# Query features of batches 1 to 3: a and b repeated by DMA through DRAM, their products as matmul weights

## The chip, the cores and the metric

The kernel runs on one core of one Trainium2 chip. Times are device microseconds of that core for one whole execution; a profile shows one such execution, and its span is a little shorter than the time of the run.

## The reference

Two blocks are chained. The first is an attention without softmax, whose features are products of two projections; the second mixes eight experts with weights that are balanced in eight rounds over rows and columns.

```python
def phi(x):                                   # (4, 4, 1088, 32) -> (4, 4, 1088, 64)
    a = np.einsum('rd,bhsd->bhsr', S1, x)     # r = 8
    b = np.einsum('rd,bhsd->bhsr', S2, x)
    return np.einsum('bhsi,bhsj->bhsij', a, b).reshape(*x.shape[:-1], r * r)
q_p, k_p = phi(q), phi(k)
kv = np.einsum('bhsf,bhsd->bhfd', k_p, v)
z = np.sum(k_p, axis=2)
num = np.einsum('bhsf,bhfd->bhsd', q_p, kv)
den = np.einsum('bhsf,bhf->bhs', q_p, z)[..., None] + 1e-06
x = (num / den).transpose(0, 2, 1, 3).reshape(4352, 128)
...
logits = x @ w_gate
P = np.exp(logits - logits.max())
for _ in range(8):
    P /= P.sum(1, keepdims=True) + 1e-09
    P /= P.sum(0, keepdims=True) + 1e-09
    P *= N / E
for e in range(8):
    out += P[:, e:e + 1] * (np.maximum(x @ w1[e], 0.0) @ w2[e])    # w1[e] 128 x 1024
```

All data are float32 (S1 and S2 arrive as float64).

## The kernel before

**Layout.** x is kept transposed in `xT`: head and dimension on the 128 partitions, the 4352 tokens along the free axis, batch after batch of S = 1088.

**Attention of one batch** (L272 to L396). `transpose_k` and `transpose_q` turn k and q with VectorE. `keys_ab` projects the keys (TensorE, weights taken from kT), ScalarE copies the projections, `keys_products` multiplies them on VectorE, and `keys_sums` (L324) sums products times v and times ones into kv and z; `keys_kept` copies these to `kvz`. The queries go in three chunks of 384, 352 and 352 tokens, with features on partitions and tokens along the free axis: `query_products` (L355) computes a and b already repeated to 64 features a head, with 64 rows and 128 columns of the array, and ScalarE copies a to `qa`; `multiply` (L367) forms the products on VectorE; `fractions` (L377) multiplies by kv and, in a second bank, by z repeated over 32 columns; `divide` (L389 to L396) takes one denominator of 32 by a transpose, forms the reciprocal, repeats it by a second transpose and multiplies into `xT`.

**Experts.** `groups` lists which tokens and experts are computed together. Seven plain groups come first (expert 0 on all tokens, expert 1 on the first 1280); their results are kept and weighted later, so they need only x. They are computed two token tiles at a time in seven products (`seven`, L973) of sums of the hidden layer's blocks; then come weighted groups of three tiles, whose x is multiplied by the routing weights beforehand. In each step `first` (L800) computes one block of the hidden layer into a bank, ScalarE applies the relu (L804), VectorE forms the sums (L817 in plain groups, L862 in groups of three), and the second layer follows `LAG` = 8 steps behind. A step of a plain group of n columns counts n/480 units. Up to three weight sets are prepared ahead at the start of an item (`prepare_w`).

**Order.** The attention is a generator with a `yield` between stages; `fill(n)` runs expert steps worth n units between them, so that TensorE has plain-group work while an attention stage waits on another engine. `counts` gives the units for each yield. Batch 0's attention comes ahead of all experts; batch 1's begins among the first fills; then `routing` runs its eight rounds with fills in between. The order on TensorE and VectorE is as written (`manual_schedule`); for SP's queue and POOL the framework chooses it, mostly as written. [...]

**Banks.** The attention and `first` take turns in the four PSUM banks of tag "a" (`bank()`, one after the other round the ring); the other four hold the second layer's sums, and before them batch 0's query products.

**Loads.** k, q and v are loaded on SP's queue: one DMA each for k and q, twelve for v. `load_kq` and `load_v` for batch 0 come first, then k and q of batch 1, the gate, expert 0's weights and v of batch 1.

```python
    def load_kq(b):
        kx = ld.tile([P, SA, D], F32, tag="k", name="kx")
        qx = ld.tile([P, SA, D], F32, tag="q", name="qx")
...
    chunks = ((0, 384), (384, 736), (736, S))
...
    counts = {1: (1, 1, 1, 1, 1, 1, 1, 1, 1), 2: (1, 1, 1, 1, 1, 1, 1, 1, 1, 1, 1, 2),
              3: (1, 1, 1, 1, 1, 1, 1, 1, 1, 1, 1, 1.25)}
```

Of the kernel before, what the change touches and what calls it, by code (L numbers as in the profile page):

```python
# [50 lines left out]
def kernel(  # L51
# [73 lines left out]
    xT = big.tile([P, N], F32, name="xT")  # L125

    lgT = wk.tile([P, SA, 32], F32, name="lgT", bufs=1)
    lgp = wk.tile([P, SA, 32], F32, name="lgp", bufs=1)
# [3 lines left out]
    summed = []  # L132
    for i in range(2):
        t = consts.tile([P, 2, 2, 2, D], F32, name=f"kvz{i}")
        nc.vector.memset(t, 0.0)
        summed.append(t)
# [9 lines left out]
    def load_kq(b):  # L146
        kx = ld.tile([P, SA, D], F32, tag="k", name="kx")
        qx = ld.tile([P, SA, D], F32, tag="q", name="qx")
        nc.sync.dma_start(out=kx, in_=k[b].rearrange("h (s a) d -> (h s) a d", a=SA))
        nc.sync.dma_start(out=qx, in_=q[b].rearrange("h (s a) d -> (h s) a d", a=SA))  # L150
        loaded[b] = kx, qx, v_slots[b % 2]
# [15 lines left out]
    load_kq(0)  # L167
    load_v(0)
    load_kq(1)
# [65 lines left out]
    wq = consts.tile([P, 2, 2, R, R], F32, name="wq")  # L235

# [15 lines left out]

    wdf = wd.rearrange("p n h r -> p (n h r)")
# [8 lines left out]
    first_w = load_w(0)  # L262
    load_v(1)
# [4 lines left out]
    def products_bank(b, i):  # L268

        return bank() if b else mps.tile([P, 512], F32, tag=f"s{i}", name="s")  # L270

    def transpose_q(b, lo=0, hi=S):  # L272
        if not lo:
            queries[b] = wk.tile([P, S], F32, tag="qT", name="qT")
        nc.vector.transpose(out=queries[b][:, lo:hi], in_=loaded[b][1].rearrange("p a d -> p (a d)")[:, lo:hi])  # L275

    def transpose_k(b):
        kx = loaded[b][0]
        kT = wk.tile([P, S], F32, tag="kT", name="kT")
# [3 lines left out]
        keys[b] = kT  # L283

    def keys_ab(b):

        kT = keys[b]
        ab = wk.tile([P, 2, NT + 1, H * R], F32, tag="ab", name="ab")
# [25 lines left out]
    def keys_sums(b):  # L314

        kp, vx = products.pop(b), loaded[b][2]
# [14 lines left out]
    def keys_kept(b):  # L331
        pv = sums_of.pop(b)

        kvz = summed[b % 2]
        for i in range(2):
            for s in range(2):
                sl = slice(64 * s, 64 * (s + 1))
                if s:
                    nc.vector.tensor_copy(kvz[sl, :, i, s, :], pv[sl, i])
                else:  # L340
                    nc.scalar.copy(kvz[sl, :, i, s, :], pv[sl, i])
        keys[b] = kvz
# [3 lines left out]
    def query_products(b, c):  # L346
# [3 lines left out]
        qT = queries[b]  # L350
        banks = [[products_bank(b, 2 * i + m) for m in range(2)] for i in range(2)]
# [5 lines left out]
        ph = []  # L357
        for i in range(2):
            qa = wk.tile([P, 384], F32, tag=f"qa{i}", name="qa")
            nc.scalar.copy(qa[:, 0:n], banks[i][0][:, 0:n])  # L360
            ph.append((qa, banks[i][1]))
        queries[b, c] = ph

    def multiply(b, c):
        n = chunks[c][1] - chunks[c][0]
        for qa, pb in queries[b, c]:
            nc.vector.tensor_tensor(qa[:, 0:n], qa[:, 0:n], pb[:, 0:n], op=Alu.mult)  # L367

    def fractions(b, c):

        n = chunks[c][1] - chunks[c][0]
        kvz = keys[b]
        ph = queries[b, c]
        pn, pd = bank(), bank()
        for t, m in ((pd, 1), (pn, 0)):
            for i in range(2):
                nc.tensor.matmul(t[64 * i:64 * (i + 1), 0:n], kvz[:, (i + m) % 2, i].rearrange("p h d -> p (h d)"),  # L377
                                 ph[i][0][:, 0:n], start=True, stop=True, tile_position=(0, 64 * i))
        queries[b, c] = pn, pd

    def divide(b, c):
# [5 lines left out]
        pn, pd = queries.pop((b, c))  # L387
# [8 lines left out]
        nc.vector.tensor_tensor(xT[:, b * S + lo:b * S + hi], pn[:, 0:n], rd[:, 0:n], op=Alu.mult)  # L396
# [16 lines left out]
    def attention(b):  # L413
# [3 lines left out]
        if b > 1:  # L417
            query_products(b, 0)
            yield
            keys_sums(b)  # L420
            multiply(b, 0)
            if follows:
                transpose_k(b + 1)
            yield
            keys_kept(b)
            fractions(b, 0)
            yield
        divide(b, 0)
        if b + 2 < B:
            load_kq(b + 2)  # L430
            load_v(b + 2)
        if follows:
            keys_ab(b + 1)
        yield
        query_products(b, 1)
        yield
        multiply(b, 1)
# [3 lines left out]
        fractions(b, 1)  # L441
        yield
        divide(b, 1)
        if follows:
            keys_products(b + 1, 0)
        yield
        query_products(b, 2)
        yield
        multiply(b, 2)
        if follows:  # L450
            keys_products(b + 1, 1)
        yield
        fractions(b, 2)
        yield
        divide(b, 2)
        if follows:
            keys_products(b + 1, 2)
        yield
# [11 lines left out]
    def routing():  # L470

        yield 0.75
# [43 lines left out]
        for b in (1, 0, 2, 3):  # L516
# [14 lines left out]
    groups = [(0, 256, 2, [0], False), *((512 + 960 * i, 480, 2, [0], False) for i in range(4)),  # L531
              (512, 384, 2, [1], False), (0, 256, 2, [1], False)]
# [14 lines left out]
    def prepare_w(j):  # L547
# [4 lines left out]
        elif items[j - 1][1] == e:  # L552
            loaded_w[j] = loaded_w[j - 1]
# [429 lines left out]
    def steps():  # L983

        todo, sums_at, t = {}, {}, 0
        for k in range(len(blocks) + 5):
# [5 lines left out]
            if k < len(blocks):  # L992
# [3 lines left out]
                if q == 0:  # L996
                    for i in (j, j + 1, j + 2 if j + 2 < first_weighted else j):
# [137 lines left out]
```

## Time and profile before

| | |
|---|---|
| median of three runs | 944.45 us (944.32 to 944.78) |
| span of the profiled execution | 942.6 us (its run: 944.38 us) |
| matmul instructions | 7170 |
| TensorE's granted clock | 0.998 |
| DMA over the span | 113.07 MB, mean 120 GB/s |
| first weighted expert matmul | 207.5 us |

In the profile PE is TensorE's matmuls and PEld its weight loads, DVE is VectorE, ACT ScalarE, POOL GpSimd, SP the engine whose queue issues most DMAs. A timeline row gives the start, the length, the engine, the line and the operation with its tiles and shapes; "128*64" is the part of the array in use, 128 rows by 64 columns, and "x8" the number of instructions merged. A float32 matmul call is two instructions. The end of a matmul is modelled and its latency is part of its length, so rows overlap; the distance from start to start is what it takes of TensorE.

### The profile page before, as it was taken

What the parts mean: (1) busy time and instruction counts of PE and PEld (TensorE: products, weight loads), DVE (VectorE), ACT (ScalarE), POOL (GpSimd) and SP (SyncE); (2) the same over time, 40 slices, a digit from 0 to 9 for tenths busy, and PEclk for the clock granted to TensorE, in tenths of its full rate; (3) what the DMA queues carried; (4) which work ended last, traced back from release to release, by engine and by line L of the source; (5) the groups of instructions that cost most, each with busy time, mean ns of one, the idle gap of its engine ahead of it and who ended that gap; (6) DMA issues with size and microseconds to landing.
All of it is one profiled execution on the core that took longest, in us unless ns stands there. A gap on an engine that the chain in (4) does not pass through costs nothing.

```text
span 942.6 us, 18270 instructions
## 1 busy us (share of the span) xinstructions
PE 928.9 (99%) x7170; PEld 556.1 (59%) x7170; DVE 702.4 (75%) x1214; ACT 419.6 (45%) x894; POOL 191.6 (20%) x176
## 2 busy tenths in 40 slices
PE   8999999999999999999999999999999999999996
PEld 6553535566666666665555555555555555556896
DVE  7787679988778788677785756975767977768665
ACT  2444445555444454444544444544445444445443
POOL 1010000063467411040011100110110343321220
PEclk9999999999999999999999999999999999999999
DMA  6600000122433454444453443454343556453640
GB/s 190 189 1 1 2 1 1 59 71 85 129 107 124 155 195 138 140 146 151 129 144 126 159 138 117 136 151 163 116 137 124 158 167 205 142 180 90 175 145 12
DMA packets 86342, 113.07 MB, mean 120 GB/s; under 512 B 23888, under 2 KB 67920, under 8 KB 81904
## 3 DMA queue, kind: packets, MB, share of 16 engines
q1 hardware_dynamic: 85024, 111.74, 38.3%
q8 instruction: 56, 0.92, 0.4%
q10 hardware_dynamic: 1232, 0.16, 0.1%
q14 instruction: 30, 0.25, 0.1%
HBM read 99.03 MB, written 12.85 MB: 119 GB/s over the span
## 4 chain that ended last, share of the span: by engine, by line
PE 94%; DVE 4%; issue 1%; ACT 1%; POOL 0%; DVEq 0%; ACTq 0%; POOLq 0%
PE a L800 48%; PE s L973 41%; PE a L355 1%; PE a L377 1%; PE a L324 1%; PE a L114 1%; DVE hb L862 1%; DVE hb L817 0%; DVE pqg L862 0%; PE a L293 0%; DVE kp L309 0%; DVE qa L367 0%; DVE qT L275 0%; PE a L402 0%; DVE rd L394 0%
## 5 line engine op out<-in xcount | busy, mean ns | idle before, releaser
L800 PE MATMUL a<-xe,w 128*64 128x256 f32 (+1 forms) x2560 | 517.8, 470 | 0.0
L804 ACT ACTIVATE hb<-a 128x256 f32<-128x256 f32 (+3 forms) x392 | 192.2, 493 | 257.8 <-PE a L800 232.8
L804 ACT ACTIVATE hx<-a 128x256 f32<-128x256 f32 (+1 forms) x360 | 167.3, 465 | 212.6 <-PE a L800 191.5
L800 PEld LDWEIGHTS a<-xe,w 128*64 128x64 f32 x2560 | 210.0, 137 | 73.2
L973 PE MATMUL s<-hb,ws 128*64 128x256 f32 (+2 forms) x1312 | 235.3, 400 | 0.1
L973 PE MATMUL s<-hx,ws 128*64 128x256 f32 x1280 | 205.4, 379 | 0.9 <-DVE kept L629 0.9
L862 DVE TENSOR_TENSOR hb<-hb 128x512 f32<-128x512 f32 (+1 forms) x204 | 131.0, 653 | 97.2 <-ACT hb L804 92.6
L862 DVE TENSOR_TENSOR hx<-hx 128x512 f32<-128x512 f32 (+1 forms) x204 | 152.5, 757 | 66.5 <-ACT hx L804 61.6
L569 POOL TENSOR_TENSOR xe<-xT,xe 128x768 f32<-128x768 f32 (+2 forms) x41 | 83.6, 2040 | 569.0 <-DMA xe<-pT 367.4
L973 PEld LDWEIGHTS s<-hb,ws 128*64 128x64 f32 x1312 | 109.0, 137 | 111.8 <-issue 85.8
L973 PEld LDWEIGHTS s<-hx,ws 128*64 128x64 f32 x1280 | 107.2, 137 | 95.4 <-issue 72.4
L800 PE MATMUL a<-xT,w 128*64 128x480 f32 (+2 forms) x448 | 121.8, 506 | 1.0 <-DVE xT L396 0.9
L973 PE MATMUL s<-hb,w 128*64 128x256 f32 (+2 forms) x472 | 100.9, 423 | 1.0 <-DVE kept L629 1.0
L817 DVE TENSOR_TENSOR hb<-hb 128x480 f32<-128x480 f32 (+5 forms) x84 | 65.8, 786 | 14.1 <-PE s L973 6.9
L973 PE MATMUL s<-hx,w 128*64 128x256 f32 x384 | 68.4, 379 | 0.0
L800 PEld LDWEIGHTS a<-xT,w 128*64 128x64 f32 x448 | 44.2, 137 | 32.8 <-issue 18.1
L225 POOL TENSOR_TENSOR ws<-w 128x256 f32<-128x256 f32 (+1 forms) x70 | 58.9, 876 | 13.1 <-PE a L800 9.8
L973 PEld LDWEIGHTS s<-hb,w 128*64 128x64 f32 x472 | 43.6, 137 | 27.9 <-issue 12.2
L817 DVE TENSOR_TENSOR hx<-hx 128x256 f32<-128x256 f32 (+1 forms) x65 | 39.5, 612 | 24.3 <-ACT hx L804 23.1
L862 DVE TENSOR_TENSOR pqg<-hb 128x512 f32<-128x512 f32 x68 | 51.3, 795 | 0.0
L973 PEld LDWEIGHTS s<-hx,w 128*64 128x64 f32 x384 | 34.4, 137 | 10.1
L862 DVE TENSOR_TENSOR pqg<-hx 128x512 f32<-128x512 f32 x68 | 35.0, 554 | 0.0
(150 smaller groups left out, 490.3 us busy)
## 6 DMA issues: line engine op xcount, KB each, us to landing
w<-in_moe_w_dram SPq DMA_DIRECT2D x82, 512.0 KB, 5.0
ws<-ws SPq DMA_DIRECT2D x34, 1024.0 KB, 5.0
xe<-pT SPq DMA_DIRECT2D x34, 384.0 KB, 3.9
ws<-ws SPq DMA_DIRECT2D x12, 512.0 KB, 4.7
pb<-pT SPq DMA_DIRECT2D x6, 384.0 KB, 6.7
kx<-in_k_dram SPq DMA_DIRECT2D x4, 544.0 KB, 4.3
qx<-in_q_dram SPq DMA_DIRECT2D x4, 544.0 KB, 5.6
v<-in_v_dram SPq DMA_DIRECT2D x32, 64.0 KB, 4.3
```

The lines of the kernel that those rows point to most:

```text
L114: nc.tensor.matmul(warm[:, 0:P], ones, ones, start=True, stop=True)
L225: tc.keep_in_program_order(nc.gpsimd.tensor_tensor(ws[:, c:c + len(ns)], blocks(x), blocks(y), op=Alu.subtract if off else Alu.add))
L324: nc.tensor.matmul(pv[64 * s:64 * (s + 1), i], kp[0:n, H * t + h].rearrange("p i j -> p (i j)"), vx[0:n, slots[h], t, :], start=(t == 0 an ...
L355: nc.tensor.matmul(banks[i][m][:, 0:n], wqf[sl, m, :], qT[sl, lo:hi], start=True, stop=True, tile_position=(64 * i, 0))
L377: nc.tensor.matmul(t[64 * i:64 * (i + 1), 0:n], kvz[:, (i + m) % 2, i].rearrange("p h d -> p (h d)"), ph[i][0][:, 0:n], start=True, stop=T ...
L569: tc.keep_in_program_order(nc.gpsimd.tensor_tensor(out, x, pb, op=Alu.mult))
L800: nc.tensor.matmul(ph[sl], loaded_w[j][0][:, P * f + H2 * s:P * f + H2 * (s + 1)], sources[j][:, lo:hi], start=True, stop=True, tile_posit ...
L804: nc.scalar.activation(out=out, in_=ph, func=Act.Relu)
L817: nc.vector.tensor_tensor(out, a, b, op=Alu.subtract)
L862: nc.vector.tensor_tensor(out if not isinstance(out, tuple) else places(*out), places(*a), places(*b) if isinstance(b, tuple) else b, op=A ...
L973: nc.tensor.matmul(sums[g][i][H2 * s:H2 * (s + 1), n * place:n * (place + 1)], w, x, start=c == 1, stop=c == per, tile_position=(0, H2 * s))
```

## The change

Batch 0 is computed as before. For batches 1 to 3 the queries are handled with tokens on partitions at the end:

- `queries_ab` projects q with one set of weights (`wdq`) for four heads; for this the 1088 tokens are padded to 1152 (`W9` = 288 blocks in each of four quarters). It stores a once and b eight times over to DRAM (`qa`, `qb`); `repeat` loads both back so that each of a's and b's rows stands where the 64 features of a head need it, b in `rb`, a in `phs`.
- `times` multiplies them on VectorE, a third of the batch at a time (768 elements a partition).
- `tops` uses those products as weights and moves the keys' sums `kvs` (two heads of 32 columns and z, 66 columns), so numerators and denominators of 64 tokens come out together, tokens on partitions; two more matmuls with ones add the 1e-6.
- `over` takes one reciprocal for each token and head, multiplies, and transposes; `take_over` stores the result to DRAM and loads it back into `xT` in the layout needed.
- The two buffers of k become one; k of batch 1 is loaded after v of batch 1, k and q of later batches after `keys_ab` or `tops`. kT and qT have one buffer each and are shared with the logits' tiles.
- The plain groups have other sizes and another order (eight of them, the same pairs of token and expert), the fills between the attention's stages are 1.4 units, and `routing` begins with a fill of 5 units. Weights of the third item aren't prepared at the first.

The diff, cut:

```diff
-    xT = big.tile([P, N], F32, name="xT")
-    lgT = wk.tile([P, SA, 32], F32, name="lgT", bufs=1)
-    lgp = wk.tile([P, SA, 32], F32, name="lgp", bufs=1)
+    xT = big.tile([P, N + 2 * 32], F32, name="xT")
+    W9 = 9 * 32
+    qT = wk.tile([P, 4 * W9], F32, name="qT", bufs=1)
+    nc.gpsimd.memset(qT[:, S:], 0.0)
+    kT = wk.tile([P, S], F32, name="kT", bufs=1)
+    phs = [wk.tile([P, 2, 4 * W9], F32, name=f"ph{i}", bufs=1) for i in range(2)]
+    rb = wk.tile([P, 2, 4 * W9], F32, name="rb", bufs=1)
+    lgT = qT[:, 0:S].rearrange("p (a s) -> p a s", s=32)
+    lgp = kT.rearrange("p (a e) -> p a e", e=32)
...
+        kvs.append(consts.tile([P, 2, 2, D + 1], F32, name=f"kvs{i}"))
...
+    eps = consts.tile([P, 3, H], F32, name="eps")
+    nc.gpsimd.memset(eps, 1e-6 / P)
...
-    load_kq(0)
+    load_k(0)
+    load_q(0)
     load_v(0)
-    load_kq(1)
...
+        nc.gpsimd.tensor_copy(wdq[:, 0], wd[:, 0].rearrange("p h r -> p (h r)"))
+        nc.gpsimd.tensor_copy(wdq[:, 1].rearrange("p (r h) -> p r h", h=H), wd[:, 1].rearrange("p h r -> p r h"))
...
     first_w = load_w(0)
+    load_q(1)
     load_v(1)
...
+    def queries_ab(b):
+        qa = dram.tile([H * R, 2, 2 * W9], F32, name=f"qa{b}")
+        qb = dram.tile([R, R * H, 2, 2 * W9], F32, name=f"qb{b}")
+        ab = wk.tile([P, 3, 192], F32, tag="qab", name="qab", bufs=1)
+        x = qT.rearrange("p (h q c t s) -> p h c t q s", h=2, q=2, c=3, t=3)
+        for cs in ((0, 1), (2,)):
+            pq = bank()[:, 0:192 * len(cs)].rearrange("p (c n) -> p c n", n=192)
+            for i, c in enumerate(cs):
+                for s in range(2):
+                    nc.tensor.matmul(pq[64 * s:64 * (s + 1), i].rearrange("p (t q s) -> p t q s", t=3, q=2),
+                                     wdq.rearrange("p n f -> p (n f)"), x[:, s, c], start=True, stop=True,
+                                     tile_position=(0, 64 * s))
+            nc.scalar.copy(ab[:, cs[0]:cs[-1] + 1], pq)
+        abf = ab.rearrange("p c n -> p (c n)")
+        for s in range(2):
+            nc.sync.dma_start(out=qb.rearrange("i f s n -> s f i n")[s],
+                              in_=abf[64 * s + 32:64 * (s + 1)].unsqueeze(1).to_broadcast([32, R, 2 * W9]))
+        for s in range(2):
+            nc.sync.dma_start(out=qa[:, s], in_=abf[64 * s:64 * s + 32])
+        queries[b] = qa, qb
+
+    def repeat(b):
+        qa, qb = queries.pop(b)
+        for h in range(2):
+            nc.sync.dma_start(out=rb[64 * h:64 * (h + 1)],
+                              in_=qb.rearrange("i (j x h) s n -> h (i j) x (s n)", x=2, h=2)[h])
+        for j in range(R):
+            nc.sync.dma_start(out=phs[b % 2][j::R], in_=qa.rearrange("(x r) s n -> r x (s n)", x=2))
...
+    def times(b, c):
+        ph = third(phs[b % 2], c)
+        nc.vector.tensor_tensor(ph, ph, third(rb, c), op=Alu.mult)
+
+    def tops(b, c):
+        pn = bank()[:, 0:3 * H * (D + 1)].rearrange("p (t h d) -> p t h d", t=3, h=H)
+        ph = third(phs[b % 2], c)
+        for t in range(3):
+            for i in range(2):
+                for s in range(2):
+                    nc.tensor.matmul(pn[64 * s:64 * (s + 1), t, 2 * i:2 * i + 2].rearrange("p h d -> p (h d)"),
+                                     ph[:, i, s, 64 * t:64 * (t + 1)], kvs[b % 2][:, i].rearrange("p h d -> p (h d)"),
+                                     start=(t == 0 and i == 0), stop=False, tile_position=(0, 64 * s))
+        for s in range(2):
+            nc.tensor.matmul(pn[64 * s:64 * (s + 1), :, :, D], ones[:, 0:64], eps, start=False, stop=True,
+                             tile_position=(0, 64 * s))
+        queries[b, c] = pn
...
+    def over(b, c):
+        pn = queries.pop((b, c))
+        rc = wk.tile([P, 12], F32, tag="rc", name="rc").rearrange("p (t h) -> p t h", h=H)
+        nc.vector.reciprocal(rc, pn[:, :, :, D])
+        xs = wk.tile([P, 384], F32, tag="rd", name="rd").rearrange("p (h t d) -> p h t d", h=H, t=3)
+        nc.vector.tensor_tensor(xs.rearrange("p h t d -> p t h d"), pn[:, :, :, 0:D],
+                                rc.unsqueeze(3).to_broadcast([P, 3, H, D]), op=Alu.mult)
...
+        nc.vector.transpose(out=turned[b][:, :, 96 * c:96 * (c + 1)].rearrange("p h (t s) -> p h t s", t=3), in_=xs)
+
+    def take_over(b, lo, hi):
+        xd = dram.tile([P, H, hi - lo], F32, name=f"xd{b}{lo}")
+        nc.sync.dma_start(out=xd, in_=turned[b][:, :, lo:hi])
+        for h in range(H):
+            nc.sync.dma_start(
+                out=xT[32 * h:32 * (h + 1), b * S:b * S + 4 * W9].rearrange("d (f n) -> d f n", f=4)[:, :, lo:hi],
+                in_=xd.rearrange("(f d) h n -> h d f n", f=4)[h])
...
     def attention(b):
         follows = b + 1 < B
...
+        keys_sums(b)
+        times(b, 0)
+        if follows:
+            transpose_q(b + 1)
+        yield
+        keys_kept(b)
+        if follows:
+            queries_ab(b + 1)
+        times(b, 1)
+        tops(b, 0)
+        yield
+        times(b, 2)
+        if follows:
+            repeat(b + 1)
+        over(b, 0)
+        tops(b, 1)
+        yield
+        over(b, 1)
+        if b + 1 == B:
+            take_over(b, 0, 192)
+        yield
+        tops(b, 2)
+        if follows:
+            transpose_k(b + 1)
+        if b + 2 < B:
+            load_k(b + 2)
+            load_q(b + 2)
+            load_v(b + 2)
+        yield
+        over(b, 2)
+        if b + 1 < B:
+            take_over(b, 0, W9)
+        else:
+            take_over(b, 192, W9)
+        if follows:
+            keys_ab(b + 1)
+            yield
+            keys_products(b + 1, 0)
+            yield
+            keys_products(b + 1, 1)
+            yield
+            keys_products(b + 1, 2)
+            yield
...
-        yield 0.75
+        yield 5
...
-    groups = [(0, 256, 2, [0], False), *((512 + 960 * i, 480, 2, [0], False) for i in range(4)),
-              (512, 384, 2, [1], False), (0, 256, 2, [1], False)]
+    groups = [(0, 256, 2, [0], False), (512, 288, 2, [0], False), (0, 256, 2, [1], False),
+              *((1088 + 960 * i, 480, 2, [0], False) for i in range(3)), (3968, 192, 2, [0], False),
+              (512, 384, 2, [1], False)]
...
         fill(1)
-        multiply(0, 2)
-        fractions(0, 2)
+        transpose_q(1)
+        queries_ab(1)
+        repeat(1)
+        multiply(2)
+        fractions(2)
         fill(1)
         transpose_k(1)
-        divide(0, 2)
+        divide(2)
         keys_ab(1)
-        fill(1)
-        transpose_q(1)
-        load_kq(2)
+        load_k(2)
+        load_q(2)
         load_v(2)
-        fill(1)
+        fill(2)
         keys_products(1, 0)
-        query_products(1, 0)
-        fill(1)
+        fill(1.5)
         keys_products(1, 1)
-        multiply(1, 0)
-        fill(1)
+        fill(1.5)
         keys_products(1, 2)
-        keys_sums(1)
-        transpose_k(2)
-        fill(1)
-        keys_kept(1)
-        fractions(1, 0)
-        fill(1)
+        fill(1.5)
         for b in range(1, B):
-            for n, _ in zip(counts[b], attention(b), strict=True):
+            for n, _ in zip((1.4,) * (9 if b + 1 < B else 5), attention(b), strict=True):
                 fill(n)
```

## Prediction

> **What bounds the kernel now.** I read the page's busy times first, then TensorE by windows, then the attention's rows in the groups kept apart by shape, then the timeline around single steps, and last the waits and SP's queue.
>
> ```profile
> PE 928.9 (99%) x7170; PEld 556.1 (59%) x7170; DVE 702.4 (75%) x1214; ACT 419.6 (45%) x894; POOL 191.6 (20%) x176
> ```
>
> ```profile
> 25.00:30.00 5.00, 3.73 (x29) 1.89 (x26) 4.93 (x7) 2.72 (x9) 0.00 (x0) 1.00 0.78 258
> 30.00:35.00 5.00, 5.00 (x100) 3.90 (x98) 3.59 (x8) 1.38 (x5) 0.00 (x0) 1.00 0.56 145
> ...
> 60.00:70.00 10.00, 10.00 (x127) 5.49 (x125) 8.10 (x19) 2.99 (x7) 0.00 (x0) 1.00 0.01 2
> ```
>
> TensorE is busy for 928.9 of 942.6 us; only before 30 us does it have gaps worth naming. So matmul time that is removed comes off the end, and an added wait costs only what TensorE can't fill. The window rows give PE, PEld, DVE, ACT and POOL busy, then clock, DMA share and GB/s: DVE is full at 25-30 us and DMA idle at 60-70 us. The change trades the first for the second.
>
> ```profile
> 59.49 1.56 PE L355 MATMUL a<-qT,wq 64*128 64x384 f32 x8
> 60.98 1.03 PE L800 MATMUL a<-xT,w 128*64 128x480 f32 x4
> ...
> 62.64 2.41 PE L324 MATMUL a<-v,kp 128*64 128x64 f32 x72
> ...
> 72.30 1.45 PE L355 MATMUL a<-qT,wq 64*128 64x352 f32 x8
> 73.70 1.03 PE L800 MATMUL a<-xT,w 128*64 128x480 f32 x4
> ...
> 76.97 1.35 PE L377 MATMUL a<-qa,kvz 128*64 128x352 f32 x8
> 78.15 0.97 PE L800 MATMUL a<-xT,w 128*64 128x480 f32 x4
> ```
>
> Each matmul call is two rows (36 calls in keys_sums, 72 rows). Ends are modelled, so I take start to next start: 1.49 and 1.40 us for the query products of 384 and 352 tokens, 1.18 for the fractions of 352, and 2.34 for 72 rows that move 64 columns, 33 ns a row.
>
> [...] L355 (64*128 among 128*64) takes 0.22 us longer than L377 with the same columns, and starts 0.1 us late as well. [...]on this kernel's SP queue 8 KB of v land in 1.9 us, and reads behind the store of pT wait 3.1 us. [...]
>
> **The change part by part, batches 1 to 3.**
>
> *Matmuls removed.* query_products: 1.49+1.40+1.40 plus 0.1 at each of three starts, 4.6 us a batch. fractions: 384/352 x 1.18 = 1.29, then 1.18 twice, 3.65 us. Together 8.25 us.
>
> *Matmuls added.* queries_ab: 6 calls, 12 rows of 192 columns; 147 ns x 192/352 = 80 ns, so 0.96 us. tops: per third 12 calls of 66 columns and 2 for eps, 28 rows at 34 ns = 0.95 us, 2.86 a batch. Together 3.8 us. The saving is 4.43 a batch, 13.3 us in all. Every saved row runs while TensorE is the bound, so I count it in full. Bounds: [...] 14.5 us (queries_ab and eps hidden in other rows' latency).
>
> *VectorE.* Removed per batch: multiply 2 x (0.55+0.52+0.52) = 3.2; divide 2.1+2.0+2.0 = 6.1. Added: times, 768 elements [...] 0.96 us, three of them 2.9; over, 0.23+0.56+0.58, three of them 4.1. It saves 2.3 us. ScalarE loses six qa copies (2.8) and gains two of about 0.5 and 0.4. Neither bounds; I count zero.
>
> *DMA added on SP's queue.* Per batch: four stores of a and b (1.33 MB), ten loads (two of rb, eight of phs: 2.36 MB), then x: one store and four loads of 0.59 MB each way. That is 4.9 MB beside the 1.67 MB of k, q and v, 33 DMAs in all. Early slices move 343 to 384 GB/s where the queue is full; I use 340.
>
> *The round trip.* From transposed queries: matmuls and copies 2 us; stores 3.9 + 1.9; loads, which wait for the stores, 6.9 + 1.9: 16.6 us until times can start. For batches 2 and 3 the order leaves eight stretches of 1.4 units. A unit is one step of 480 columns with its products, 1.6 us (73.70 to 75.36, 0.85+0.81), and about 5 us of attention matmuls lie between: 23 us, so it is hidden. For batch 1: queries_ab at 21.7 us (after DVE's divide and the 1.3 us transpose), times(1, 0) behind 7.5 units and keys_ab: 37.8 by my walk. That is 16.1 us, half a us short. Behind it on SP comes q of batch 2 (k first: 1.1 MB, 3.3 us), which transpose_q(2) needs right after times(1, 0). So DVE stands about 4 us, with the expert's sums queued behind. TensorE waits for those sums, but products run LAG = 8 steps late and the sums are issued 4 to 5 steps after their block begins: 3 steps of 0.8 us (256 columns), 2.4 us, are hidden. I take 2.0 us lost. Bounds: 0 (SP's instructions are not all in program order; k and q may come earlier) and 9 (the 12 DMAs of v, which took SP from 12.4 to 23 us for batch 1, stand before the stores).
>
> *k of batch 1 later.* It moves from 10.0 us on SP to behind v of batch 1, at about 21.3; plus the 4.3 us of the kx row, 25.6. transpose_k(1) ends at 27.0 and keys_ab(1) starts at 26.9 instead of 23.1. On DVE, divide(2) and the first sums wait behind it; on TensorE, all. Filled by queries_ab, fractions(2) and fill(1); about 2 us stay idle, and 0.9 more before the first sums. Before has 1.27 us there (L355 waiting for qT), which goes. Net 1.6 us, bounds 0 and 4.
>
> *Banks.* tops holds one of four "a" banks until over has read it; four allocations later TensorE stands if DVE is late. Before took four at once with 4.9 us of weight-load idling behind ACT qa, nearly all hidden. I take +1.0, bounds -0.5 and +5.
>
> *logits.* The last third of batch 3 goes store (3.1), four loads issued at 0.4 and landing in 1.9 (3.5), after over (1.4) and a DVE lag of about 1: 9.0 us, against fill(5) = 5 x 1.5 (early rate) = 7.5. I take +1.5, bounds 0 and 3.
>
> *Groups.* Same token-expert pairs and columns, but eight plain groups for seven; one more turnover of the sums. The shown one cost 0.97 us (L973 waiting for kept); I take +0.5, bounds 0 and 1.2. Expert 1's weights are needed sooner, and 1 MB (3.1 us) rides in the DMA bound. Routing ends some 3 units closer to its first use, which had 25 us (182 to 207.5): nothing. The memsets and copies on POOL lie in its idle time before 20.9 us: nothing.
>
> **Sum.** -13.3 + 2.0 + 1.6 + 1.0 + 1.5 + 0.5 = -6.7 us. Against its own span, 942.6, that is 935.9; the profiled run was 944.38 and the median 944.45, so the time is 937.7.
>
> **Rivals.**
>
> *Everything hides.* Only the saving and the extra turnover count: -12.8, 931.6; with the upper saving 930. For it: DMA is idle from 50 us and DVE gets lighter. Against: before 45 us DMA is 25 to 95% busy already.
>
> *tops waits for banks.* Nine thirds at 1 us each instead of 1.0 in all: +8, 945.7, no change. For it: early steps have 256 or 288 columns, so 1.4 units are two or three banks. Against: before survived four banks at once.
>
> *The round trip through DRAM is the bound (slower).* Place: times(b, 0), the first VectorE instruction that reads rb and phs. Price: batch 1 loses its 9 us of bound. Batches 2 and 3 run late once the 3.69 MB need more than 23 - 5.8 = 17 us, that is, under 215 GB/s. At 150 GB/s, near the 170 GB/s of 40-45 us where v loads are in flight, they take 24.6 us: 7.4 late each. 9 + 2 x 7.4 = 24 us of waiting on VectorE, less 2.4 hidden three times, is 17 us; 17 - 13.3 + 4.6 = +8.3, 952.7. Against it: the full queue moves 340. For it: two dependent trips a batch in one queue, with 14 DMAs of k, q and v between them, and 16 or 32 partitions only in 16 of the 19 new DMAs.
>
> **How the numbers follow.** The chief forecast, part of the saving returned, 0.58, own range 932 to 942; all hidden 0.14; banks or other waits eat it 0.10; round trip bound 0.18. What a measurement can tell from no change is about 0.2%, 1.9 us. Faster 0.72, same 0.09, slower 0.19. The range leaves out half of the best case's tail and the worse half of the round trip: 930.5 to 949.
>
> **What would show it.** Right: PE busy falls by about 13 us and the idle before 60 us grows by 3 to 6; L355 and L377 keep only batch 0; the rows of tops stand 33 to 35 ns apart; VectorE waits for the DMA of rb or phs once, at times(1, 0), and for qx behind it. Wrong: tops rows over 45 ns apart, waits for phs in batches 2 and 3, TensorE's weight loads waiting for xs or rc (banks), or a wait over 3 us in front of L402's logits. No waits for DMA after 30 us would make the best case true. Over 944 us, the saving wasn't there or the trip ate it.

## The result, and the profile after

| | before | after |
|---|---|---|
| median | 944.51 us (944.32 to 944.78) | 951.15 us (949.96 to 952.04) |
| ratio | | 1.0069, 95% interval 1.0052 to 1.0087 |
| span of the profiled execution | 942.6 us | 949.6 us |
| TensorE busy, idle | 928.9, 13.7 us | 920.1, 29.5 us |
| granted clock | 0.998 | 0.990 |
| first weighted expert matmul | 207.5 us | 212.9 us |

The change is slower by 6.6 us; 937.7 was forecast. TensorE's busy time falls by 8.8 us, its idle time grows by 15.8, and the difference is the 7.0 us of the span. By the first weighted expert matmul 5.3 of them are lost; where the rest goes stays open. First the page's busy times after the change:

```profile
PE 920.1 (97%) x7434; PEld 554.6 (58%) x7434; DVE 692.8 (73%) x1204; ACT 417.8 (44%) x905; POOL 195.3 (21%) x182
```

The window rows (columns as in the prediction) show where the new idle time lies:

```profile
25.00:30.00 5.00, 1.69 (x35) 1.55 (x34) 2.75 (x6) 0.55 (x2) 0.00 (x0) 0.88 0.96 296
30.00:35.00 5.00, 5.00 (x43) 3.58 (x42) 4.52 (x8) 2.99 (x8) 0.00 (x0) 0.78 0.61 147
35.00:40.00 5.00, 5.00 (x66) 4.04 (x63) 3.05 (x6) 2.28 (x6) 0.00 (x0) 1.00 1.05 215
40.00:45.00 5.00, 3.77 (x73) 2.64 (x68) 0.00 (x0) 1.11 (x5) 0.00 (x0) 1.00 1.01 244
45.00:50.00 5.00, 0.00 (x0) 0.00 (x0) 2.15 (x2) 0.00 (x0) 0.00 (x0) 0.58 0.66 189
50.00:55.00 5.00, 4.73 (x46) 3.94 (x48) 2.81 (x7) 0.80 (x2) 0.00 (x0) 0.50 0.69 193
...
100.00:110.00 10.00, 6.43 (x93) 3.83 (x89) 4.27 (x8) 3.85 (x11) 0.00 (x0) 1.00 0.73 175
110.00:120.00 10.00, 9.49 (x88) 5.38 (x89) 7.93 (x15) 2.05 (x4) 0.00 (x0) 0.83 0.35 98
```

TensorE stops three times for over 3 us, in front of 28.5, 50.3 and 110.5 us. After each stop the granted clock (the third number from the end) is below 1 in the next rows: 0.78, 0.50 and 0.83. From 35 to 45 us the DMA engines are busy all the time and yet move only 215 and 244 GB/s. What ends the stops stands in the timelines of VectorE, then of TensorE:

```profile
27.09 1.25 DVE L295 STREAM_TRANSPOSE kT<-kx 128x1024 f32<-128x1024 f32 x1 [4.47 <-DMA kx<-in_k_dram]
45.60 0.96 DVE L451 TENSOR_TENSOR ph<-ph,rb 128x768 f32<-128x768 f32 x1 [7.16 <-DMA kx<-in_k_dram]
48.81 1.31 DVE L291 STREAM_TRANSPOSE qT<-qx 128x1088 f32<-128x1088 f32 x1 [2.26 <-DMA qx<-in_q_dram]
...
107.04 0.96 DVE L451 TENSOR_TENSOR ph<-ph,rb 128x768 f32<-128x768 f32 x1 [5.66 <-DMA xd<-xt]
```

```profile
28.48 1.78 PE L306 MATMUL a<-wd,kT 128*64 128x64 f32 x32 [3.31 <-DVE kT L297]
50.27 2.19 PE L426 MATMUL a<-qT,wdq 128*64 128x192 f32 x12 [6.50 <-DVE qT L291]
...
110.51 1.49 PE L460 MATMUL a<-kvs,ph 128*64 128x66 f32 x24 [4.09 <-DVE kvs L359]
```

L451 is `times`, for batch 1 at 45.60 us and for batch 3 at 107.04. It reads neither kx nor xd: those names are only what landed last. What it needs are `rb` and `phs`, and the last packets of `phs` ran until 44.5 us. The load of q of batch 2 stands behind them on SP's queue, its transpose behind `times` on VectorE, and `queries_ab` (L426) at the head of TensorE's queue waits for that. For batch 3, `tops` (L460) waits for the copy into `kvs`, which stands behind `times` on VectorE: the last rows of `keys_sums` (L337) ended at 103.4 us, ScalarE copied its part at 103.48 and VectorE its own at 110.00. The loads themselves, in the DMA view from 30 to 46 us (the kind of tile, DMAs, KB each, median us to landing):

```profile
rb<-qb SPq DMA_DIRECT2D x2, 576.0 KB, 5.6
ph<-qa SPq DMA_DIRECT2D x8, 144.0 KB, 7.6
```

### The profile page after: what moved, and what is told of

Read it like the earlier page. It is cut to its first block, busy times and chain, and to the rows that moved or that the text cites. A ratio compares the mean times of both kernels' runs of the same rounds, so it can differ in the third digit from the quotient of the medians.

```text
span 949.6 us, 18935 instructions
## 1 busy us (share of the span) xinstructions
PE 920.1 (97%) x7434; PEld 554.6 (58%) x7434; DVE 692.8 (73%) x1204; ACT 417.8 (44%) x905; POOL 195.3 (21%) x182
## 4 chain that ended last, share of the span: by engine, by line
PE 86%; DVE 6%; DMA 5%; issue 1%; ACT 1%; SPq 1%; POOL 0%; DVEq 0%; ACTq 0%
PE a L895 45%; PE s L1068 39%; DMA rb<-qb 2%; DMA qx<-in_q_dram 1%; DVE hb L912 1%; DMA w<-in_moe_w_dram 1%; DMA qb<-qab 1%; PE a L460 1%; DVE hb L957 1%; DMA xd<-xt 0%; PE a L426 0%; DVE pqg L957 0%; PE a L337 0%; DVE kept L721 0%; DVE cs L594 0%
## 5 line engine op out<-in xcount | busy, mean ns | idle before, releaser
L899 ACT ACTIVATE hb<-a 128x256 f32<-128x256 f32 (+5 forms) x408 | 195.2, 480 | 260.5 <-PE a L895 235.1
L895 PEld LDWEIGHTS a<-xe,w 128*64 128x64 f32 x2560 | 207.7, 137 | 79.3 <-issue 2.2
L1068 PE MATMUL s<-hb,ws 128*64 128x256 f32 (+4 forms) x1344 | 239.1, 395 | 2.1 <-DVE hb L912 1.6
L957 DVE TENSOR_TENSOR hb<-hb 128x512 f32<-128x512 f32 (+1 forms) x204 | 133.4, 665 | 94.3 <-ACT hb L899 90.3
L1068 PEld LDWEIGHTS s<-hb,ws 128*64 128x64 f32 x1344 | 113.9, 137 | 111.5 <-issue 82.3
L895 PE MATMUL a<-xT,w 128*64 128x480 f32 (+4 forms) x512 | 123.0, 475 | 1.0 <-DVE xT L410 0.9
L1068 PE MATMUL s<-hb,w 128*64 128x256 f32 (+4 forms) x496 | 102.1, 412 | 1.8 <-DVE kept L724 1.8
L912 DVE TENSOR_TENSOR hb<-hb 128x480 f32<-128x480 f32 (+8 forms) x96 | 64.5, 673 | 20.6 <-ACT hb L899 11.0
L895 PEld LDWEIGHTS a<-xT,w 128*64 128x64 f32 x512 | 51.3, 141 | 28.3 <-issue 17.6
L957 DVE TENSOR_TENSOR pqg<-hb 128x512 f32<-128x512 f32 x68 | 48.3, 750 | 0.0
L957 DVE TENSOR_TENSOR pqg<-hx 128x512 f32<-128x512 f32 x68 | 35.8, 566 | 0.0
```

Of the source, the lines that this page charges most:

```text
L895: nc.tensor.matmul(ph[sl], loaded_w[j][0][:, P * f + H2 * s:P * f + H2 * (s + 1)], sources[j][:, lo:hi], start=True, stop=True, tile_posit ...
L899: nc.scalar.activation(out=out, in_=ph, func=Act.Relu)
L912: nc.vector.tensor_tensor(out, a, b, op=Alu.subtract)
L957: nc.vector.tensor_tensor(out if not isinstance(out, tuple) else places(*out), places(*a), places(*b) if isinstance(b, tuple) else b, op=A ...
L1068: nc.tensor.matmul(sums[g][i][H2 * s:H2 * (s + 1), n * place:n * (place + 1)], w, x, start=c == 1, stop=c == per, tile_position=(0, H2 * s))
```

## The experiments

Where nothing else is said the median of the kernel before in the same runs was 944.5 to 945.0 us; ratios are to it. Medians of one kernel taken in two sittings can so differ by half a us, and differences of 1 or 2 us between two experiments are hardly clear of the noise. Piece times are medians of the DMA packets in the trace. The pieces of `rb` and `phs` have 4608 B in the change; `rb` has pieces of 9216 B in the second experiment, in the eighth, the ninth, the eleventh and the twelfth.

**Without the loads.** It leaves out the ten loads of `rb` and `phs`, which hold ones, so the attention of batches 1 to 3 isn't the reference's.

```diff
-        for h in range(2):
-            nc.sync.dma_start(out=rb[64 * h:64 * (h + 1)], ...
-        for j in range(R):
-            nc.sync.dma_start(out=phs[b % 2][j::R], ...
...
+    for t_ in (*phs, rb):
+        nc.gpsimd.memset(t_, 1.0)
```

> Leaves out the ten loads of rb and phs in each batch (both hold ones instead, so the queries' features are wrong); the stores, the loads of k, q, v and the trip of x stay. Theory A, that the trip through DRAM holds times(1, 0) and times(3, 0) and that TensorE's clock is halved for some us after each stop: the stops at 44 to 50 us and 106 to 110 us go with their slow stretches, the time falls by 13 to 17 us against the changed kernel, to about 936, and is below the kernel before by 6 to 10 us. Rival B, that the matmul saving of 13 us isn't there (tops slower than thought, banks, more groups): the time stays above 945.

Measured: 936.55 us, ratio 0.9905 (0.9891 to 0.9920), 14.6 us below the change. TensorE's busy time is 916.2 us, 12.7 below before. The windows of this kernel have no second or third stop:

```profile
40.00:45.00 5.00, 5.00 (x102) 4.09 (x98) 3.71 (x7) 1.53 (x6) 0.00 (x0) 1.00 0.45 81
45.00:50.00 5.00, 5.00 (x88) 3.98 (x86) 2.25 (x5) 2.62 (x7) 0.80 (x1) 1.00 0.99 317
...
100.00:110.00 10.00, 10.00 (x98) 5.32 (x96) 8.66 (x16) 2.85 (x5) 0.00 (x0) 1.00 0.18 53
```

So the matmul saving is there, and the loads cost more than all of it. `times(1, 0)` starts at 38.84 us here.

**Without the wait for the stores.** The same bytes go to the same places, but are read from the experts' weights instead of `qa` and `qb`, so the loads needn't wait for the stores; `rb` comes in pieces of twice the size. The values of batches 1 to 3 aren't the reference's.

```diff
-                              in_=qa.rearrange("(x r) s n -> r x (s n)", x=2))
+                              in_=AP(tensor=w, offset=294912, ap=[[1152, 16], [16 * 1152, 2], [1, 1152]]))
```

> The loads of rb and phs read as many bytes in the same pieces, but from the expert weights in DRAM, so they need not wait for the stores (the features are wrong). Theory A1, that the wait for the stores to land in DRAM is what makes the trip long: loads are issued from 25 us on, the stop at 44 to 50 us shrinks by 6 us and the time falls by 6 to 9 us. Theory A2, that the rate of the transfers is what counts (all engines busy at 210 GB/s while phs is loaded): the loads end at most 2 to 3 us earlier, the time falls by less than 4 us.

Measured: 948.74 us, ratio 1.0043 (1.0026 to 1.0059): the wait for the stores is worth 2.4 us of the 14.6. The first piece of the loads of batch 1 came only 0.7 us earlier (31.5 instead of 32.2 us). The pieces of `phs` still took 310 to 390 ns, those of `rb`, of 9216 B, 670 to 690. The rate of the loads is the greater part.

**k of batch 1 early.**

```diff
+        kx = (wk.tile([P, SA, D], F32, tag="xt", name="kx", bufs=1) if b == 1 else ...
     load_v(0)
+    load_k(1)
```

> k of batch 1 is loaded right behind v of batch 0 again, as before the change, into the buffer that xt uses later. Theory A, that the chain runs through the DMA trip, which starts at transpose_q(1) whatever k does: the stop of 3.3 us before keys_ab(1) and its slow stretch go, but the stop at 44 us begins earlier and ends within 2 us of where it did; the time falls by 0 to 3 us. Rival C, that the stops add up: it falls by 5 us.

Measured: 951.93 us, ratio 1.0070 (1.0055 to 1.0085), no gain. The stop at 25 us was gone, and the next one longer by 4.1 us:

```profile
51.94 2.19 PE L428 MATMUL a<-qT,wdq 128*64 128x192 f32 x12 [10.65 <-DVE qT L293]
```

But the trip had shifted too: `queries_ab(1)` began at 22.92 us instead of 21.93, and `times(1, 0)` at 47.11 instead of 45.60. So this run alone doesn't show that k's wait is free.

**phs in two DMAs of 128 partitions,** from a source that is repeated eight times by its access pattern.

```diff
-        for j in range(R):
-            nc.sync.dma_start(out=phs[b % 2][j::R], in_=qa.rearrange("(x r) s n -> r x (s n)", x=2))
+        for x in range(2):
+            nc.sync.dma_start(out=phs[b % 2][:, x], in_=qr[x].unsqueeze(1).to_broadcast([2 * R, R, 4 * W9]))
```

> phs is loaded by two DMAs of 128 partitions each in place of eight of 16 partitions, the same bytes. Theory D1, that the form of the eight (16 partitions, two pieces an engine) makes them slow: the 1.18 MB take 3.5 to 4 us in place of 5.8, and q of batch 2 is issued 6 us earlier; times(1, 0) starts 2 to 4 us earlier and the time falls by 3 to 7 us. Theory D2, that reading the same 147 KB eight times makes them slow whatever the form: the rate stays near 210 GB/s and the time falls by less than 2 us.

Measured: 950.10 us, ratio 1.0053 (1.0038 to 1.0068); the pieces of `phs` still took 290 to 375 ns. q of batch 2 was issued at 34.99 us instead of 40.74, and yet its transpose began at 48.55 instead of 48.81: fewer issues on SP's queue didn't help, and reaching 128 partitions in one DMA didn't either. In this execution the stop at 25 us had shrunk to 0.4 us, `times(1, 0)` started at 45.41, nearly as in the change, and the next stop grew from 6.5 to 8.6 us. As long as the trip ends when it does, TensorE only waits in another place.

**Both loads in the order of the partitions.** As the second experiment, but `rb` and `phs` are one DMA each, whose outermost step is one partition and one row of a plain source. Same bytes, all in pieces of 4608 B; each byte is read once, where the second experiment reads those of `phs` eight times. The values are again not the reference's.

```diff
+        for t_, o in ((rb, 0), (phs[b % 2], 294912)):
+            nc.sync.dma_start(out=t_, in_=AP(tensor=w, offset=o, ap=[[1152, 128], [147456, 2], [1, 1152]]))
```

> As the run whose loads of rb and phs read the expert weights and don't wait for the stores (the features are wrong here too), with the same bytes in the same pieces of 4608 B, but rb and phs come in one DMA of 128 partitions each whose outer step is one partition, as k and q are loaded. Theory P, that a load [...] (64 partitions, or every eighth) moves at half the rate: a piece takes 170 to 190 ns in place of 350, the loads end some 5 us earlier, times(1, 0) starts near 39 us, and the time is 6 to 10 us below that run, near 940. Theory H, that reading DRAM in pieces of this size or beside the stores is slow: pieces stay over 300 ns and the time within 2 us of that run.

Measured: 939.80 us, ratio 0.9942 (0.9923 to 0.9962), 8.9 us below the second experiment. Every 64 packets of these loads have a median of 178 ns. In its windows the same busy engines move 425 GB/s instead of 215:

```profile
35.00:40.00 5.00, 5.00 (x100) 3.95 (x98) 2.44 (x5) 1.46 (x6) 0.00 (x0) 1.00 1.03 425
```

Against the 178 ns stand 310 to 390 for `phs` in the second experiment. What differs for both tiles is which partitions a load reaches and in what order: the fast ones all 128, row after row, the slow ones `rb[64h:64h+64]`, one half, or `phs[j::8]`, every eighth. The evidence is best for `rb`, whose bytes are read once each in every run: pieces of 9216 B took 670 to 690 ns into one half of the partitions (second experiment, two DMAs) and 347 ns into all 128 in order (eighth, one DMA). Why the half is slower wasn't shown.

For `phs` a rival stands. In the change and in the second and fourth experiments its loads read the same 147 KB eight times over, in the fifth and eighth each byte once, and only there are they fast. The fourth reached 128 partitions and stayed slow. Either its form is slow in another way, or the repeated reading is slow by itself; no run keeps the two apart.

**TensorE kept busy through the stops** by matmuls of ones into banks that nobody reads: 15, 30 and 18 pairs in front of `keys_ab(1)`, `queries_ab(2)` and `tops(3, 0)`.

```diff
+            for s in range(2):
+                nc.tensor.matmul(w[64 * s:64 * (s + 1)], ones[:, 0:64], ones, start=True, stop=True, ...
```

> The changed kernel with idle matmuls of ones into a bank of their own (nothing reads them) ahead of keys_ab(1), queries_ab(2) and tops(3, 0), 3 to 7 us each, where TensorE stood waiting. Nothing is left out. Theory A, that each stop costs its length and then a stretch at half clock (28.5 to 32, 50 to 55 and 110.5 to 114 us): the clock stays at 1.0 there, and the time falls by 4 to 6 us to about 946. Rival W, that the slow stretches cost nothing since DMA or VectorE sets the pace there: it falls by less than 1.5 us.

Measured: 950.15 us, ratio 1.0056 (1.0041 to 1.0071), 1.0 us below the change, which the intervals don't tell from nothing. Windows of this kernel:

```profile
25.00:30.00 5.00, 4.96 (x102) 4.74 (x101) 4.22 (x9) 0.86 (x3) 0.00 (x0) 1.00 0.89 252
...
50.00:55.00 5.00, 3.64 (x44) 3.00 (x46) 3.31 (x7) 0.70 (x2) 0.00 (x0) 0.70 0.60 145
...
110.00:120.00 10.00, 10.00 (x127) 6.80 (x125) 9.58 (x19) 2.28 (x4) 0.00 (x0) 1.00 0.29 80
```

The clock is back at 1 in the first and third place, not in the second, where the ones ended before `queries_ab` began. The 4 to 6 us that I had expected didn't come. But the ones also stood in the way at the first place: kT was there at 26.9 us, and `keys_ab` (L306) began 1.7 us later, behind them:

```profile
26.70 0.20 DVE L297 STREAM_TRANSPOSE kT<-kx 128x64 f32<-128x64 f32 x1
...
28.59 1.10 PE L306 MATMUL a<-wd,kT 128*64 128x64 f32 x32
```

So what the slow clock costs stays open: one place wasn't cured, and in another the cure had its own price.

**Another order on SP's queue.** k of batch 1 early, k and q of batch 2 ahead of v of batch 1.

```diff
     load_q(1)
-    load_v(1)
...
         transpose_q(0, chunks[0][1])
+        load_k(2)
+        load_q(2)
+        load_v(1)
```

> Only the order of loads on SP's queue is changed: k of batch 1 early as in the run before, k and q of batch 2 ahead of v of batch 1, so that nothing but v of batch 2 stands behind the trip of batch 1 and neither k nor q moves during it. Nothing is left out. Theory A (the trip and q behind it set the pace until 50 us): q of batch 2 is there when times(1, 0) ends, queries_ab(2) starts near 45 us in place of 50.3, and the time falls by 4 to 8 us. Rival R, that only the rate of rb and phs counts: times(1, 0) starts within 1.5 us of 45.6 and the time falls by under 3 us.

Measured: 951.16 us, ratio 1.0065 (1.0050 to 1.0080), no gain. The twelve DMAs of v held SP until 26.8 us; the first store left at 27.81 instead of 23.57, and TensorE's stop was 12.19 us.

**Plain loads for the true values.** a is stored eight times as well, in rows in the order of the partitions, and each of `rb` and `phs` is one plain DMA. From here on nothing is left out of the computation.

```diff
+        nc.sync.dma_start(out=rb, in_=qb.rearrange("h i (j x) s n -> (h i j) x (s n)", x=2))
+        nc.sync.dma_start(out=phs[b % 2], in_=qa.rearrange("(x r) j s n -> (r j) x (s n)", x=2))
```

> The whole computation, with a too stored eight times, in rows laid out so that rb and phs are each read by one DMA into 128 partitions in the order of the rows, instead of the ten DMAs [...]. The stores of a grow from 0.15 to 1.18 MB a batch, by some 230 pieces of 2304 B at 93 ns on 16 engines for each of the two stores, +2.6 us a round trip; b leaves by four stores of 16 partitions instead of two of 32. Theory P [...]: the pieces of rb and ph fall from 315-370 to about 180 ns, the two loads from 12.8 to 5.7 us, the wait for the stores (2.4 us by e2) stays: 942 to 945 us against 951.15 for the change, so about level with the kernel before (944.9). Rival B (the bytes through DRAM are the bound[...]): the stores take what the loads give back, 948 to 952. A third outcome, the pieces of the stores far over 93 ns because 16 partitions are too few, would also give 947 or more and show in the packets.

Measured: 948.91 us, ratio 1.0046 (1.0031 to 1.0061), in the rival's range. The pieces of `phs` fell to 178 ns, those of `rb`, of 9216 B, took 347, and the loads of batch 1 ran for 9.7 us (34.7 to 44.4) instead of 12.3 (32.2 to 44.5). But the stores now ran from 25.5 to 35.8 us instead of 25.3 to 31.7: 1.03 MB more, and their pieces of 2304 B at 93 to 185 ns instead of mostly 93. `times(1, 0)` started at 44.79 instead of 45.60 us. The fast loads of the fifth experiment weren't to be had at its price, because these rows have to be written first.

**The same with k early** and v of batch 1 behind the repeat.

```diff
     load_v(0)
+    load_k(1)
...
         repeat(1)
+        load_v(1)
```

> As e8_both_whole, and k of batch 1 is loaded behind v of batch 0 (into the turned output's buffer) and v of batch 1 behind the repeat of batch 1, so that neither the keys' sketch nor the stores of a and b wait for SP. e3 and e7 moved the loads of k without a gain while the loads of rb and phs were slow. Theory C (a chain through the trip hid the late k, and with a faster trip the 3.3 us stop at 25 us costs its length): 1.5 to 3.5 us under e8_both_whole, 939 to 943. Rival (the trip is still the bound of this stage): within 0.7 us of e8_both_whole.

Measured: 949.58 us, ratio 1.0050 (1.0032 to 1.0068), as the one before within the intervals. The stop at 25 us was gone, but `keys_sums(1)` (L338) now stood for v of batch 1, which had gone behind the loads, and `times(1, 0)` started at 46.07 us instead of 44.79:

```profile
46.22 0.48 PE L338 MATMUL a<-v,kp 64*64 64x64 f32 x4 [7.27 <-DMA v<-in_v_dram]
```

So the run put one wait in the place of another, and doesn't test k alone.

**More expert work ahead of the trip's end.** The DMAs of the change; only the order on TensorE differs.

```diff
-    groups = [(0, 256, 2, [0], False), (512, 288, 2, [0], False), (0, 256, 2, [1], False),
+    groups = [(0, 256, 2, [0], False), (512, 288, 2, [0], False), (0, 256, 2, [1], False), (512, 288, 2, [1], False),
               *((1088 + 960 * i, 480, 2, [0], False) for i in range(3)), (3968, 192, 2, [0], False),
-              (512, 384, 2, [1], False)]
+              (1088, 96, 2, [1], False)]
...
-        fill(2)
+        fill(3.2)
...
-            for n, _ in zip((1.4,) * (9 if b + 1 < B else 5), attention(b), strict=True):
+            for n, _ in zip((0.9,) * 9 if b == 1 else (1.75,) * 9 if b == 2 else (0.8,) * 5, attention(b), strict=True):
```

The three fills of 1.5 around the keys' products became 2.8, 2.8 and 2.7.

> The DMAs of the change as they are; only the order on TensorE differs. Expert 1's products on tokens 512 to 1088 (batch 0) come ahead of the first group that needs batch 1, and some 5 shares more of expert products (1.6 us a share) are put between the keys' sketch of batch 1 and its sums, as many fewer into batch 1's own attention; some 3 shares more go into batch 2's attention, fewer into batch 3's. Theory F (the stops are work of the trip at the head of an in-order engine with expert products ready behind it): the stops at 44 to 50 us and at 106 to 110 us (7.2 and 5.7 us by DVE's wait) go or fall under 2 us; with the 3.3 us stop at 25 us left, 940 to 945 us. Rival T (the trip is the bound of the whole stage): the stop only moves, to the first product on batch 1's tokens near 83 us or to the logits near 128 us; 948 to 952.

Measured: 949.67 us, ratio 1.0059 (1.0040 to 1.0078). The time is in the range of the rival, but the picture is neither theory's: the stop at 44 us fell by half and that at 106 us went, but a new one came at 76 us, at batch 2's trip, whose fills I had taken away:

```profile
50.93 2.06 PE L426 MATMUL a<-qT,wdq 128*64 128x192 f32 x12 [3.31 <-DVE qT L291]
...
81.41 2.19 PE L426 MATMUL a<-qT,wdq 128*64 128x192 f32 x12 [5.36 <-DVE qT L291]
```

**That order with the plain loads.**

```diff
+        nc.sync.dma_start(out=rb, in_=qb.rearrange("h i (j x) s n -> (h i j) x (s n)", x=2))
...
+        fill(3.2)
```

> The order of e10_more_fill with the stores and loads of e8_both_whole (a stored eight times, two plain loads of 128 partitions). Theory F: as e10_more_fill or up to 2 us better, 939 to 944, since what the faster loads give (2.2 us in e8) lies under expert products. Rival T: as e8_both_whole, 947 to 950.

Measured: 945.51 us, ratio 1.0010 (0.9998 to 1.0022), between the two expectations. The same two rows:

```profile
48.94 1.20 PE L426 MATMUL a<-qT,wdq 128*64 128x192 f32 x12 [1.21 <-DVE qT L291]
...
76.58 2.19 PE L426 MATMUL a<-qT,wdq 128*64 128x192 f32 x12 [2.59 <-DVE qT L291]
```

Here the plain loads gave 4.2 us (against the tenth experiment), where in the order of the change they gave 2.2 (the eighth): `times(1, 0)` started 2.3 us earlier and `times(2, 0)` 5.2.

**The fills balanced, k early.**

```diff
-            for n, _ in zip((0.9,) * 9 if b == 1 else ...
+            for n, _ in zip((1.3,) * 9 if b == 1 else ...
```

> As e11_fill_whole with batch 1's attention given 1.3 shares of expert products at each of its nine places instead of 0.9, and k of batch 1 loaded behind v of batch 0. In e11 the stop at 44 us was gone, but the 2.6 us stop at 74 us (the sketch of q of batch 3 behind batch 2's trip) was new, the granted clock was 0.81 and 0.84 from 70 to 90 us, and TensorE still waited 1.6 us for k of batch 1 at 25 us; the first 480-token product began at 103.8 us, 20 us after its tokens were there, so there is work to put ahead. Theory F: both stops go, about 4 us of waits and 1 to 2 us of clock: 940 to 943.5 us, below the kernel before (944.6). Rival (a stop that is filled only appears at the next trip, or the later groups lose it): 944.5 to 947.

Measured: 940.92 us (939.57 to 942.19), ratio 0.9960 (0.9946 to 0.9973): below both kernels, 3.8 us under the one before. Its page and windows:

```profile
PE 917.1 (98%) x7554; PEld 569.5 (61%) x7554; DVE 700.4 (75%) x1222; ACT 420.0 (45%) x928; POOL 192.0 (20%) x182
```

```profile
25.00:30.00 5.00, 5.00 (x68) 3.83 (x66) 3.47 (x8) 2.54 (x9) 0.00 (x0) 0.92 0.63 127
...
45.00:50.00 5.00, 4.04 (x53) 2.40 (x47) 1.39 (x2) 1.73 (x6) 0.00 (x0) 1.00 0.64 204
50.00:55.00 5.00, 2.46 (x35) 2.17 (x37) 4.80 (x10) 0.70 (x2) 0.00 (x0) 0.81 0.54 153
...
100.00:110.00 10.00, 10.00 (x132) 7.17 (x130) 7.78 (x14) 4.66 (x12) 0.00 (x0) 1.00 0.68 228
```

The stop at 25 us and those at the trips of batches 2 and 3 are gone. What is left are 2.0 us ahead of `queries_ab(1)` at 23 us and 3.5 us around 50 us. How the 4.6 us against the eleventh divide between its two edits wasn't tried, nor what the regrouping would do for the kernel before.

## Why the prediction was wrong

**The step that failed is the round trip,** sized "loads, which wait for the stores, 6.9 + 1.9: 16.6 us until times can start", and from it "16.1 us, half a us short" for batch 1 and "23 us, so it is hidden" for batches 2 and 3. From `queries_ab(1)` at 21.93 us to `times(1, 0)` at 45.60 are 23.7 us. The rows of SP's queue divide them:

```profile
23.57 0.80 SPq L432 DMA_DIRECT2D qb<-qab  x2
...
30.84 1.24 SPq L441 DMA_DIRECT2D rb<-qb  x2
```

Matmuls and copies took 1.6 us (2 forecast), the stores until the first load could be issued 7.3 (5.8), and from there to `times` 14.8 us (8.8). The loads' pieces ran for 12.3 us, which for 2.36 MB is 192 GB/s instead of the 340 I took from slices in which k, q and the weights arrive. Those go to 128 partitions in order, and pieces of 4352 B of k and q took 168 ns before 6 us; the new loads don't, and their pieces of 4608 B took 349 (medians), twice as long. I had named the "16 or 32 partitions only" in a rival and priced it at nothing in the forecast. The time that the order leaves was right for batch 1: VectorE had come to `times(1, 0)` at 38.4 us (45.60 less its wait of 7.16), 37.8 forecast.

For batch 3 the trip took 26.3 us (80.77 to 107.04) against the 23 that I said the order leaves, and the order left less: VectorE was there 20.6 us after `queries_ab(3)` (107.04 less its wait of 5.66). Part of the trip's length is SP's queue: in its timeline the second store of b stands behind the loads of x, which wait for the store of `xd`:

```profile
81.09 0.37 SPq L484 DMA_DIRECT2D xd<-xt  x1
83.33 0.31 SPq L432 DMA_DIRECT2D qb<-qab  x1
83.93 3.44 SPq L486 DMA_DIRECT2D xT<-xd  x4
87.41 1.24 SPq L432 DMA_DIRECT2D qb<-qab  x1
```

Batch 2's trip was hidden, as forecast: 27.6 us passed (50.27 to 77.87), and its loads had ended at 74.5. The tenth experiment, with fewer fills beside it, shows how little was to spare.

**What the loads cost.** Against the kernel without loads: 2.4 us for the wait for the stores (second experiment), 8.9 for the slow pieces (fifth against second; the partitions reached and their order, and for `phs` perhaps the repeated reading) and 3.2 for the rest, the bytes themselves and what queues behind them (fifth against first, 939.80 - 936.55). That is 14.6 us where the forecast had 2.0. The three add up by construction, since each is the difference of two runs next to each other in this row.

**The rival that ended on the other side** gave 952.7; 951.15 was measured. Its place, `times(b, 0)`, and its cause are right. Its rate of 150 GB/s for all three batches is not: the loads of batch 1 ran at 192, and one batch of three was hidden. Its sum had 21.6 us of added waits (17 + 4.6) and 13.3 of busy time saved; TensorE's idle time grew by 15.8 and its busy time fell by 8.8. The two errors nearly cancel, so that the number came so near is luck.

**Matmuls:** -13.3 us forecast (its 147 ns a row are the 1.18 us over eight rows of 352 columns), -12.7 in the busy time of the kernel without loads. In the change only -8.8 shows: its matmuls are busy for 3.9 us more than those without loads (920.1 - 916.2), and the clock after its stops (0.50 from 50 to 55 us) is the likely reason. A third of `tops` took less than forecast, in TensorE's timeline 24 rows in 0.70 us, 29 ns a row instead of 34:

```profile
114.62 0.90 PE L460 MATMUL a<-kvs,ph 128*64 128x66 f32 x24
115.32 0.27 PE L464 MATMUL a<-eps,ones 128*64 128x12 f32 x4
```

**k of batch 1 later:** 1.6 us forecast, and a stop of 3.3 us came. But it isn't a term of a sum: in the fourth experiment it shrank to 0.4 us, and the stop behind the trip grew by 2.1; the third and ninth, which meant to remove it, shifted other things as well.

**Banks and logits:** 1.0 and 1.5 us forecast, both below 1. `tops` made no weight load wait over 1.0 us for a bank, and no stop shows between 120 and 130 us ahead of the logits. VectorE got lighter by 9.6 us (7 forecast by its terms; 0.96 us was forecast for one `times`, and 0.96 measured) and wasn't the bound. The turnover of the extra group can't be told apart.

**Missing from the sum: the clock.** After stops of 3.3, 6.5 and 4.1 us the clock fell to 0.78, 0.50 and 0.83 in the windows; in windows cut finer it was 0.50 from 29 to 32, from 46 to 56 and from 112 to 114 us. But the length of the stop alone doesn't decide here: in the twelfth experiment the rows of `queries_ab` took 2.19 us behind a stop of 2.02 (at 23.01 us) and 1.20 behind one of 1.99 (at 51.03), and in the eighth the clock was 1.00 from 25 to 30 us, with a stop of 2.4. What it cost in time isn't shown: with two of three places cured, 1.0 us came back, within the noise.

## What to carry to other kernels

Price a DMA by the partitions it reaches, in its order, and by how often it reads the same bytes, and not by the rate of whole-tile loads: pieces of one size took 178 or some 350 ns here. A trip through DRAM is free only if the in-order queues (SP, VectorE, TensorE) have work in front of what waits for it (batch 2's 27.6 us cost no stop here, batch 1's 23.7 one of 6.5); where the trip sets the end of a stage, removing other waits only moves the stop. The fix that paid was of both kinds at once, shorter loads and independent matmuls moved ahead, and each alone gave some 2 us, hardly clear of the noise. What the regrouping alone would give the kernel before isn't known, so the 3.7 us under it need not come from the change.

## What the runs showed of the hardware

- Stores from 32 partitions ran mostly at 93 ns for 2304 B, as fast a byte as the best loads (178 ns for 4608 B). For batch 3 of the change most took 185 ns, and in the eighth experiment they varied between 93 and 185; what slows them wasn't tried.
- DMA engines that are shown 100% busy moved 215 GB/s in one run and 425 in another (35 to 40 us of the change and of the fifth experiment): the busy share says nothing of the rate.
- A matmul row that moves 66 columns and follows others of its kind takes 29 ns from start to start (24 rows in 0.70 us).
